# Attention of two batches ahead of a SwiGLU FFN: a new load order, and down projections held back, in a fused one-core kernel

## Chip, cores, metric

One core of one Trainium2 chip. The metric is the device time of one execution in microseconds (us). Medians are quoted with their range; every comparison is made by ratio to runs of the kernel before.

## The reference

Block-causal attention over 8 batches, 8 heads, 576 tokens and head size 64, then a root-mean-square norm and a SwiGLU FFN on 4608 tokens of width 512 with an inner width of 1536. Everything comes and goes in float32.

```python
scores = (q @ k^T) / sqrt(64)             # token i sees token j if i//64 >= j//64
x      = softmax(scores) @ v              # (8, 8, 576, 64) -> (4608, 512)
xn     = x / sqrt(mean(x*x) + 1e-6) * rms_g
g      = xn @ w_gate
out    = (g * sigmoid(g) * (xn @ w_val)) @ w_out
```

## The kernel before

The kernel emits its own schedule: the order of the Python calls is the order of the instructions on each engine. Tiles carry the waits. The parts that matter:

```python
NST = 6                                         # staging tiles for loads (fp32)
nat    = pool(bufs=10)                          # bf16 tiles after the cast on GpSimd
ps_s   = pool(bufs=2)   # PSUM: scores, values    ps_f = pool(bufs=4)   # PSUM: FFN, norm, transposes

def issue(): ...        # next load of the list `todo`, on Sync's queue
def cast(eng, n=1):     # oldest staged tile to bf16, then issue() into the freed staging tile
    ...
def transpose_pair(b, t): ...  # TensorE transposes, VectorE copies to QT/KT     (batches 0 and 1)
def transpose_dma(b, c):  ...  # DMA transposes on Sync's queue                  (other batches)
def scores(b, t, step):   ...  # 3 steps a head pair; exp on ScalarE; corner memsets on VectorE

def values(b, t, early=False):
    ...                                         # 10 matmuls into ov[:, 0, :]
    out(OT[b][:, t, 0:512], SQ[b][:, t, 0:512], ov[:, 0, :])    # two ScalarE passes
    if t == HP - 1:
        for u in range(HP):                     # end blocks, into ov[:, 1, :] of the same tile
            for a in range(2):
                nc.tensor.matmul(ov[a*D:(a+1)*D, 1, u*BLK:(u+1)*BLK], ...)
        out(OT[b][:, :, 512:S], SQ[b][:, :, 512:S], ov[:, 1, 0:HP*BLK]...)

def ffn_up(n, m):   ...  # 8 matmuls, tanh on ScalarE, two multiplies on VectorE
def ffn_down(n, i): ...  # 12 matmuls, ScalarE copy to osb, then
    nc.sync.dma_start(out=out[rows[0]:rows[0] + P, :], in_=osb)

def group():             # one FFN step: a down if due, else an up if its tokens are normed, else a down
    ready = di < len(downs) and (ui == len(ups) or downs[di][0]*NMC + NMC + 2 <= ui)
    if ready and (ui == len(ups) or 3*di <= ui - NMC - 3): ffn_down(*downs[di]); di += 1
    elif ui < len(ups) and <last batch of the chunk> < scaled: ffn_up(*ups[ui]); ui += 1
    elif di < len(downs) and downs[di][0]*NMC + NMC <= ui: ffn_down(*downs[di]); di += 1
    gone += 1; <run what `later` has set for this count>

def tail(b):             # norm of a batch, spread over the next five groups
    norm_sums(b, 0); norm_sums(b, 1); later(1, norm_root, b)
    for u in range(HP + 1): later(3 + u//2, norm_scale, b, u)
    later(3 + HP//2, mark, b)                   # only now may up steps use batch b
```

The order before: attention of batch 0 (up weights issued beside its V), norm of batch 0 with nothing beside it, then FFN groups between the attention steps of batches 1 to 7. A group without a step that may run is empty.

The softmax here doesn't subtract the row's maximum and nothing guards it: scores larger than these inputs give would overflow.

## Time and profile before

| | before |
|---|---|
| time, 2 runs | 441.5 us (441.24 to 441.77) |
| profiled span | 441.4 us, mean granted clock 0.974 |
| TensorE busy | 388.4 us (88%) |
| loads, transposes and stores on Sync's queue | 45.9 MB |

The prediction below quotes the page, the table of stretches and TensorE's timeline, and says how to read them. In a timeline line the numbers are the start, the length, then what ran, and in brackets how long the engine had been idle and who ended it.

### The profile page before, as it was taken

The page shows a single profiled execution, that of the slowest core. Times are in us where ns is not written, and L with a number is a line of the kernel's source. Part 1 is how long each engine was busy: PE and PEld are TensorE (multiplying, and loading weights), DVE is VectorE, ACT ScalarE, POOL GpSimd, SP SyncE. Part 2 cuts the span into 40 slices and gives each one's busy share as a digit, 9 for nine tenths or more (in the row PEclk, how much of TensorE's full clock was granted, in tenths as well). Part 3 has the DMA queues.
Part 4 walks back from the last instruction along what each step waited for, and adds up shares of the span by engine and source line. Part 5 has one row for each costly group of instructions (what it writes and reads, how often), then busy time and mean ns, then how long its engine had stood idle before and what let it go on. Part 6 is the DMA issues. An engine that isn't in the chain of part 4 may idle for free.

```text
span 441.4 us, 7178 instructions
## 1 busy us (share of the span) xinstructions
PE 388.4 (88%) x2661; PEld 172.7 (39%) x2704; DVE 249.0 (56%) x593; ACT 216.3 (49%) x322; POOL 86.1 (20%) x138
## 2 busy tenths in 40 slices
PE   3535679985998999899989998999899989999995
PEld 1213343332344434443444444444444444444442
DVE  4615875506665466546654665566546665776430
ACT  3503147643765466546754675467546732333221
POOL 2547243332241023201320232011000000000000
PEclk9999589997999999999999999999999999999998
DMA  8999999987990499349936982492011002000012
GB/s 207 166 233 228 209 194 147 188 206 150 169 185 0 108 202 173 57 107 192 182 57 105 197 184 55 107 185 43 1 61 37 1 0 73 24 1 24 24 50 95
DMA packets 142708, 51.08 MB, mean 116 GB/s; under 512 B 129360, under 2 KB 138064, under 8 KB 142672
## 3 DMA queue, kind: packets, MB, share of 16 engines
q1 hardware_dynamic: 136320, 45.89, 51.4%
q0 software_dynamic: 5824, 4.72, 6.8%
q8 instruction: 21, 0.34, 0.3%
q14 instruction: 15, 0.12, 0.1%
q10 hardware_dynamic: 528, 0.00, 0.1%
HBM read 38.80 MB, written 9.44 MB: 109 GB/s over the span
## 4 chain that ended last, share of the span: by engine, by line
PE 81%; DMA 7%; ACT 4%; DVE 4%; POOL 1%; issue 1%; SPq 0%; DVEq 0%; POOLq 0%; ACTq 0%
PE fps L415 22%; PE fps L431 21%; PE fps L419 21%; PE sps L248 6%; PE sps L288 4%; DMA st<-in_k_dram 3%; DMA st<-in_v_dram 2%; PE fps L324 2%; ACT PT L254 2%; DMA WO<-in_moe_w_out_dram 2%; PE fps L396 2%; ACT SQ L299 1%; DVE QT L222 1%; ACT OT L298 1%; DVE KT L222 1%
## 5 line engine op out<-in xcount | busy, mean ns | idle before, releaser
L254 ACT ACTIVATE PT<-sps 128x1024 bf16<-128x1024 f32 (+1 forms) x96 | 93.9, 988 | 66.7 <-PE sps L248 65.7
L424 DVE SCALAR_TENSOR_TENSOR gs<-th,fps 128x512 bf16<-128x512 f32 x108 | 74.3, 688 | 75.4 <-ACT th L422 74.7
L415 PE MATMUL fps<-XT,WG 128*128 128x512 bf16 x408 | 111.0, 385 | 1.5 <-issue 0.5
L419 PE MATMUL fps<-XT,WV 128*128 128x512 bf16 x430 | 112.1, 383 | 0.2
L431 PE MATMUL fps<-WO,HT 128*128 128x512 bf16 x417 | 96.9, 379 | 0.8
L422 ACT ACTIVATE th<-fps 128x512 f32<-128x512 f32 x108 | 64.9, 601 | 64.9 <-PE fps L415 62.8
L426 DVE TENSOR_TENSOR HT<-gs,fps 128x512 bf16<-128x512 bf16 x108 | 74.2, 687 | 11.5 <-PE fps L419 0.4
L419 PEld LDWEIGHTS <-WV 128*128 128x128 bf16 x432 | 42.7, 99 | 52.3 <-issue 2.3
L431 PEld LDWEIGHTS <-HT 128*128 128x128 bf16 x432 | 40.7, 98 | 49.8 <-issue 3.5
L145 POOL CAST nt<-st 128x512 bf16<-128x512 f32 (+1 forms) x60 | 36.8, 615 | 111.9 <-DMA st<-in_k_dram 88.7
L434 ACT ACTIVATE osb<-fps 128x512 f32<-128x512 f32 x36 | 21.5, 597 | 71.7 <-PE fps L431 58.7
L415 PEld LDWEIGHTS <-WG 128*128 128x128 bf16 x432 | 37.2, 98 | 47.1 <-issue 11.7
L389 DVE SCALAR_TENSOR_TENSOR XT<-OT,gscale,fps 128x64 bf16<-128x64 bf16 (+3 forms) x72 | 30.2, 476 | 30.8 <-PE fps L396 27.7
L248 PE MATMUL sps<-QT,KT 64*128 64x512 bf16 (+3 forms) x256 | 38.4, 341 | 3.3 <-DVE KT L222 1.6
L288 PE MATMUL sps<-PT,VB 128*64 128x512 bf16 (+3 forms) x256 | 27.3, 338 | 0.0
L138 POOL CAST VB<-st 128x512 bf16<-128x512 f32 x24 | 14.8, 615 | 53.3 <-DMA st<-in_v_dram 50.6
L248 PEld LDWEIGHTS <-KT 64*128 64x128 bf16 x256 | 9.9, 94 | 35.2 <-issue 31.0
L288 PEld LDWEIGHTS <-VB 128*64 128x64 bf16 x320 | 13.8, 114 | 22.9 <-POOL VB L140 8.7
L299 ACT ACTIVATE SQ<-sps 128x512 bf16<-128x512 f32 (+1 forms) x37 | 20.9, 565 | 2.9 <-DVE OT L293 2.9
L298 ACT CAST OT<-sps 128x512 bf16<-128x512 f32 (+1 forms) x35 | 18.8, 538 | 4.3 <-PE sps L306 2.8
L396 PE MATMUL fps<-st,SELB 128*128 128x512 bf16 x30 | 10.2, 426 | 7.9 <-DVE st L378 7.6
L215 PE MATMUL fps<-ident,nt 96*128 96x96 bf16 x96 | 7.7, 246 | 8.4 <-DVE nt L128 7.9
(69 smaller groups left out, 184.9 us busy)
## 6 DMA issues: line engine op xcount, KB each, us to landing
out_dram<-osb SPq DMA_DIRECT2D x28, 256.0 KB, 2.3
st<-in_q_dram SPq DMA_DIRECT2D x24, 256.0 KB, 4.5
st<-in_k_dram SPq DMA_DIRECT2D x24, 256.0 KB, 4.9
st<-in_v_dram SPq DMA_DIRECT2D x24, 256.0 KB, 4.0
st<-in_v_dram SPq DMA_DIRECT2D x32, 128.0 KB, 5.3
st<-in_q_dram SPq DMA_DIRECT2D x8, 288.0 KB, 6.6
st<-in_k_dram SPq DMA_DIRECT2D x8, 288.0 KB, 7.0
out_dram<-osb SPq DMA_DIRECT2D x16, 128.0 KB, 2.4
```

Of the source, the lines that this page charges most:

```text
L145: eng.tensor_copy(out=nt[0:r, 0:512], in_=st[0:r, 0:512])
L248: nc.tensor.matmul(sp[:, a, o:o + CH_W[c]], KT[b][r, t, c * P:(c + 1) * P], QT[b][r, t, CH_Q[c]:S], start=True, stop=True, skip_group_chec ...
L254: nc.scalar.activation(out=pt[:, :, lo:lo + width], in_=sp[:, :, 0:width], func=AF.Exp, scale=SCALE)
L288: nc.tensor.matmul(ov[a * D:(a + 1) * D, 0, 512 - w:512], vb[:, c, h * D:(h + 1) * D], rhs, start=(c == 4), stop=(c == 3), skip_group_chec ...
L299: nc.scalar.activation(out=sq, in_=i, func=AF.Square)
L389: nc.vector.scalar_tensor_tensor(out=XT[:, u, y0:y0 + hi - lo], in0=OT[b][:, u, j0 + lo:j0 + hi], scalar=gscale[:, u:u + 1], in1=src[:, lo ...
L415: nc.tensor.matmul(g, WG[m // 3][:, p, (m % 3) * P:(m % 3 + 1) * P], XT[:, p, x0:x0 + TOKC], start=(p == 0), stop=(p == HP - 1))
L419: nc.tensor.matmul(u, WV[m // 3][:, p, (m % 3) * P:(m % 3 + 1) * P], XT[:, p, x0:x0 + TOKC], start=(p == 0), stop=(p == HP - 1))
L422: nc.scalar.activation(out=th, in_=g, func=AF.Tanh, scale=0.5)
L424: nc.vector.scalar_tensor_tensor(out=gs, in0=th, scalar=1.0, in1=g, op0=ALU.add, op1=ALU.mult)
L426: nc.vector.tensor_mul(out=HT[n][:, m, :], in0=gs, in1=u)
L431: nc.tensor.matmul(po, HT[n][:, m, i * P:(i + 1) * P], WO[:, m, :], start=(m == 0), stop=(m == NMC - 1))
```

## The change

Its intent: fill the thin first 112 us. Batch 0's V no longer shares the DMA engines with weights; the attention of batches 0 and 1 fills TensorE while the weights arrive; batch 2 is loaded and transposed as batches 0 and 1 are; the down projections wait for weights that come last.

```diff
-    def issue():
+    def issue(behind=None):            # optionally waits for a weight tile before the load
-            todo += [("vp", b, t) for t in range(HP)] + [("v", b, 4)]
+            todo += [("v", b, 4)] + [("vp", b, t) for t in range(HP)]    # and for 3 batches, not 2
@@ scores: corner memsets are gathered and issued a group later
-            nc.vector.memset(pt[BLK:P, :, 512:512 + BLK], 0.0)
+            corners.append((gone, pt[BLK:P, :, o:o + BLK]))
@@ values: end-block matmuls come before the copies; batch 0 uses ps_f instead of ps_s
-        out(OT[b][:, t, 0:512], SQ[b][:, t, 0:512], ov[:, 0, :])
+        outs = [(OT[b][:, t, 0:512], SQ[b][:, t, 0:512], ov)]
         if t == HP - 1:
             ... end-block matmuls ...
-            out(...)
+            outs.append(...)
+        for o, sq, i in outs: <copy and square>
@@ norm_root
-        for i in range(3):
+        for i in range(2):
@@ group
-        ready = di < len(downs) and downs[di][0]*NMC + NMC + 2 <= ui       # (cut)
+        ready = di < len(downs) and downs[di][0]*NMC + NMC + 2 <= ui and ui >= DOWN0    # DOWN0 = 20
@@ order (cut)
+    <attention of batch 0, batch 1's transposes and scores between its pieces, norm of batch 0>
+    cast(nc.gpsimd, 2, refill=False); load_up(0); load_up(1)
+    cast(nc.gpsimd, 3, refill=False); load_up(2); load_up(3)
+    <rest of batch 1's scores, values(1, 0..2)>; group(); values(1, 3); later(1, tail, 1)
+    while len(flying) < NST: issue(behind=WV[3][0:1, 0, 0:1])     # batch 2 behind the up weights
+    group(6)
+    for t in range(HP):                 # batch 2: transposes, scores, values; 16 groups between
+        if t < 3: transpose_pair(2, t)
+        if t == 2: transpose_pair(2, 3); scores_ends(2)
+        ...                             # load_out (down weights) at t == 2, step 1
+    values(2, 3); later(1, tail, 2)
+    later(1, transpose_dma, 3, 0)       # batch 3's DMA transposes start here
+    for _ in range(6):
+        group(); fetch(3); fetch(3)     # fetch: cast on GpSimd; every second one a DMA transpose
     <batches 3 to 7 as before>
```

More of the change, by code (lines that the diff above doesn't have):

```diff
@@ L54 @@
     NST = 6
+    NPE = 3
     const = ctx.enter_context(tc.tile_pool(name="const", bufs=1))
@@ L98, in issue @@
         st = stage.tile([P, 6 * P], FP32, name="st")
+        if behind is not None:
+            nc.gpsimd.tensor_copy(out=st[0:1, 0:1], in_=behind)
         src = {"q": q, "k": k, "v": v}[kind[0]]
@@ L119, in issue, with cast @@
         flying.append(((kind, b, i), st))
-    def cast(eng, n=1):
+    def cast(eng, n=1, refill=True):
         for _ in range(n):
@@ L145, in cast @@
                 eng.tensor_copy(out=nt[0:r, 0:512], in_=st[0:r, 0:512])
-            issue()
+            if refill:
+                issue()
     for b in range(B):
-        if b < 2:
+        if b < NPE:
             for t in range(HP):
                 todo += [("qp", b, t), ("kp", b, t)]
-            todo += [("vp", b, t) for t in range(HP)] + [("v", b, 4)]
+            todo += [("v", b, 4)] + [("vp", b, t) for t in range(HP)]
         else:
@@ L233, with clear @@
     PT, P4, OT, SQ = {}, {}, {}, {}
+    corners = []
+    gone = 0
+    def clear(age=0):
+        while corners and corners[0][0] <= gone - age:
+            nc.vector.memset(corners.pop(0)[1], 0.0)
     def scores(b, t, step):
@@ L255, in scores @@
                              func=AF.Exp, scale=SCALE)
-        if step == 1:
-            nc.vector.memset(pt[BLK:P, :, 512:512 + BLK], 0.0)
-        if step == 2:
-            for o in (960, 1280):
-                nc.vector.memset(pt[BLK:P, :, o:o + BLK], 0.0)
+        for o in ((), (512,), (960, 1280))[step]:
+            corners.append((gone, pt[BLK:P, :, o:o + BLK]))
     def scores_ends(b):
@@ L281, in values @@
         vb = VB[b % NV]
-        ov = ps_s.tile([P, 2, 512], FP32, name="sps")
+        if early:
+            ov = ps_f.tile([P, 512], FP32, name="fps")
+            oh = ps_f.tile([P, 512], FP32, name="fps") if t == HP - 1 else None
+        else:
+            ob = ps_s.tile([P, 2, 512], FP32, name="sps")
+            ov, oh = ob[:, 0, :], ob[:, 1, :]
         for c in (4, 0, 1, 2, 3):
@@ L287, in values @@
                 w = CH_W[c] if c < 4 else BLK
-                nc.tensor.matmul(ov[a * D:(a + 1) * D, 0, 512 - w:512],
+                nc.tensor.matmul(ov[a * D:(a + 1) * D, 512 - w:512],
                                  vb[:, c, h * D:(h + 1) * D], rhs,
                                  start=(c == 4), stop=(c == 3), skip_group_check=True)
-        def out(o, sq, i):
-            if early:
-                nc.vector.tensor_copy(out=o, in_=i)
-                if t < HP - 1:
-                    nc.vector.tensor_mul(out=sq, in0=o, in1=o)
-                    return
-            else:
-                nc.scalar.copy(out=o, in_=i)
-            nc.scalar.activation(out=sq, in_=i, func=AF.Square)
-        out(OT[b][:, t, 0:512], SQ[b][:, t, 0:512], ov[:, 0, :])
+        outs = [(OT[b][:, t, 0:512], SQ[b][:, t, 0:512], ov)]
         if t == HP - 1:
@@ L305, in values @@
                     h = 2 * u + a
-                    nc.tensor.matmul(ov[a * D:(a + 1) * D, 1, u * BLK:(u + 1) * BLK],
+                    nc.tensor.matmul(oh[a * D:(a + 1) * D, u * BLK:(u + 1) * BLK],
                                      vb[:, 5, h * D:(h + 1) * D], P4[b][:, a, u, :],
                                      start=True, stop=True, skip_group_check=True)
-            out(OT[b][:, :, 512:S], SQ[b][:, :, 512:S],
-                ov[:, 1, 0:HP * BLK].rearrange("p (t d) -> p t d", t=HP))
+            outs.append((OT[b][:, :, 512:S], SQ[b][:, :, 512:S],
+                         oh[:, 0:HP * BLK].rearrange("p (t d) -> p t d", t=HP)))
+        for o, sq, i in outs:
+            if early:
+                nc.vector.tensor_copy(out=o, in_=i)
+                nc.vector.tensor_mul(out=sq, in0=o, in1=o)
+            else:
+                nc.scalar.copy(out=o, in_=i)
+                nc.scalar.activation(out=sq, in_=i, func=AF.Square)
     nrm = {}
@@ L446, in ffn_down @@
                                   in_=osb[j * BLK:(j + 1) * BLK, :])
-    late_constants()
-    def casts_early(t):
-        cast(nc.vector)
-        cast(nc.gpsimd)
-    casts_early(0)
-    transpose_pair(0, 0, k_on_act=True)
-    scores(0, 0, 0)
-    casts_early(1)
-    scores(0, 0, 1)
-    transpose_pair(0, 1)
-    scores(0, 0, 2)
-    casts_early(2)
-    scores(0, 1, 0)
-    scores(0, 1, 1)
-    transpose_pair(0, 2)
-    casts_early(3)
-    scores(0, 1, 2)
-    load_up(0)
-    transpose_pair(0, 3)
-    scores(0, 2, 0)
-    cast(nc.gpsimd, 1)
-    load_up(1)
-    scores_ends(0)
-    cast(nc.gpsimd, 4)
-    scores(0, 2, 1)
-    values(0, 0, early=True)
-    scores(0, 2, 2)
-    values(0, 1, early=True)
-    scores(0, 3, 0)
-    scores(0, 3, 1)
-    values(0, 2, early=True)
-    scores(0, 3, 2)
-    norm_sums(0, 0)
-    values(0, 3, early=True)
-    norm_sums(0, 1)
-    load_up(2)
-    load_up(3)
-    norm_root(0)
-    for t in range(HP + 1):
-        norm_scale(0, t)
-    pairs = [(b, t) for b in range(1, B) for t in range(HP)]
     ups = [(n, m) for n in range(NTC) for m in range(NMC)]
     downs = [(n, i) for n in range(NTC) for i in range(4)]
-    ui = di = gone = 0
-    scaled = 1
+    ui = di = 0
+    scaled = 0
     due = []
+    DOWN0 = 20
     def later(after, fn, *args):
@@ L504, in mark, with group @@
         scaled = b + 1
-    def group():
+    def group(n=1):
         nonlocal ui, di, gone
-        ready = di < len(downs) and (ui == len(ups) or downs[di][0] * NMC + NMC + 2 <= ui)
-        if ready and (ui == len(ups) or 3 * di <= ui - NMC - 3):
-            ffn_down(*downs[di])
-            di += 1
-        elif ui < len(ups) and min(B - 1, ((ups[ui][0] + 1) * TOKC - 1) // S) < scaled:
-            ffn_up(*ups[ui])
-            ui += 1
-        elif di < len(downs) and downs[di][0] * NMC + NMC <= ui:
-            ffn_down(*downs[di])
-            di += 1
-        gone += 1
-        now = [d for d in due if d[0] <= gone]
-        due[:] = [d for d in due if d[0] > gone]
-        for _, fn, args in now:
-            fn(*args)
+        for _ in range(n):
+            ready = di < len(downs) and downs[di][0] * NMC + NMC + 2 <= ui and ui >= DOWN0
+            if ready and (ui == len(ups) or 3 * di <= ui - NMC - 3):
+                ffn_down(*downs[di])
+                di += 1
+            elif ui < len(ups) and min(B - 1, ((ups[ui][0] + 1) * TOKC - 1) // S) < scaled:
+                ffn_up(*ups[ui])
+                ui += 1
+            elif di < len(downs) and downs[di][0] * NMC + NMC <= ui:
+                ffn_down(*downs[di])
+                di += 1
+            gone += 1
+            clear(1)
+            now = [d for d in due if d[0] <= gone]
+            due[:] = [d for d in due if d[0] > gone]
+            for _, fn, args in now:
+                fn(*args)
     def tail(b):
@@ L531, in tail, with pair_in @@
         later(3 + HP // 2, mark, b)
-    cast(nc.gpsimd, 2)
-    group()
-    cast(nc.gpsimd, 2)
-    transpose_pair(1, 0)
-    cast(nc.gpsimd, 2)
-    group()
-    transpose_pair(1, 1)
-    cast(nc.gpsimd, 2)
-    for m in range(0, NMC, 3):
-        load_out(m, 3)
-    cast(nc.gpsimd, 5)
-    fetched = []
+    late_constants()
+    def pair_in(b, t):
+        cast(nc.vector if b == 0 else nc.gpsimd)
+        cast(nc.gpsimd)
+        transpose_pair(b, t, k_on_act=(b == 0 and t == 0))
+    pair_in(0, 0)
@@ new lines @@
+    scores(0, 0, 0)
+    scores(0, 0, 1)
+    pair_in(0, 1)
+    scores(0, 0, 2)
+    scores(0, 1, 0)
+    pair_in(0, 2)
+    scores(0, 1, 1)
+    scores(0, 1, 2)
+    pair_in(0, 3)
+    clear()
+    scores(0, 2, 0)
+    cast(nc.gpsimd, 5)
+    scores(0, 2, 1)
+    scores_ends(0)
+    scores(0, 2, 2)
+    clear()
+    values(0, 0, early=True)
+    scores(0, 3, 0)
+    values(0, 1, early=True)
+    scores(0, 3, 1)
+    pair_in(1, 0)
+    values(0, 2, early=True)
+    scores(0, 3, 2)
+    scores(1, 0, 0)
@@ new lines @@
+    clear()
+    norm_sums(0, 0)
+    values(0, 3, early=True)
+    norm_sums(0, 1)
+    scores(1, 0, 1)
+    pair_in(1, 1)
+    scores(1, 0, 2)
+    norm_root(0)
+    scores(1, 1, 0)
+    pair_in(1, 2)
+    scores(1, 1, 1)
+    for u in range(HP + 1):
+        norm_scale(0, u)
+    mark(0)
+    scores(1, 1, 2)
+    pair_in(1, 3)
+    clear()
+    scores(1, 2, 0)
+    cast(nc.gpsimd, 2, refill=False)
+    for j in range(2):
+        load_up(j)
+    cast(nc.gpsimd, 3, refill=False)
+    for j in range(2, 4):
+        load_up(j)
@@ new lines @@
+    scores_ends(1)
+    scores(1, 2, 1)
+    scores(1, 2, 2)
+    scores(1, 3, 0)
+    scores(1, 3, 1)
+    clear()
+    scores(1, 3, 2)
+    values(1, 0)
+    values(1, 1)
+    values(1, 2)
+    group()
+    clear()
+    values(1, 3)
+    later(1, tail, 1)
+    while len(flying) < NST:
+        issue(behind=WV[3][0:1, 0, 0:1])
+    cast(nc.gpsimd, 2)
+    group(6)
+    for t in range(HP):
+        if t < 3:
+            transpose_pair(2, t)
+        if t == 2:
+            transpose_pair(2, 3)
+            scores_ends(2)
+        for step in range(3):
+            scores(2, t, step)
+            if t == 2 and step > 0:
+                values(2, step - 1)
+            if t == 3 and step == 1:
+                values(2, 2)
+            if step == 0:
+                cast(nc.gpsimd, (2, 4, 3, 2)[t])
+            if t == 2 and step == 1:
+                cast(nc.gpsimd, 2)
+                for m in range(0, NMC, 3):
+                    load_out(m, 3)
+            group()
+        group()
@@ L548, in fetch @@
+    values(2, 3)
+    later(1, tail, 2)
+    fetched = 2
     def fetch(b):
-        n = len(fetched)
-        if n < 15 and b < B:
+        nonlocal fetched
+        if fetched < 15 and b < B:
             cast(nc.gpsimd)
-            fetched.append(n)
-            if n % 2 == 1 and n < 10:
-                later(1, transpose_dma, b, n // 2)
-    for idx, (b, t) in enumerate(pairs):
-        prev = pairs[idx - 1] if idx else None
-        if t == 0:
-            del fetched[:]
-            if b == 1:
-                scores(b, 0, 0)
-                group()
-                transpose_pair(1, 2)
-                scores(b, 0, 1)
-                group()
-                transpose_pair(1, 3)
-                scores(b, 0, 2)
-                scores_ends(1)
-                group()
-                continue
+            fetched += 1
+            if fetched % 2 == 0 and fetched <= 10:
+                later(1, transpose_dma, b, fetched // 2 - 1)
@@ L572 @@
+    later(1, transpose_dma, 3, 0)
+    for _ in range(6):
+        group()
+        fetch(3)
+        fetch(3)
+    pairs = [(b, t) for b in range(3, B) for t in range(HP)]
+    for b, t in pairs:
+        if t == 0:
+            while fetched < 15:
+                fetch(b)
+            fetched = 0
             scores_ends(b)
@@ L574 @@
         scores(b, t, 0)
-        if prev:
-            values(*prev)
-            if prev[1] == HP - 1:
-                later(1, tail, prev[0])
+        if (b, t) != pairs[0]:
+            values(*((b, t - 1) if t else (b - 1, HP - 1)))
+            if t == 0:
+                later(1, tail, b - 1)
         fetch(b + 1)
@@ L586 @@
         scores(b, t, 2)
-        group()
-        if b > 1:
-            group()
+        group(2)
         fetch(b + 1)
```

## The prediction

> **What bounds the kernel now.** I began with the page: TensorE's share of the span, then the row of forty slices, to see whether that share is even.
>
> ```profile
> PE 388.4 (88%) x2661; PEld 172.7 (39%) x2704; DVE 249.0 (56%) x593; ACT 216.3 (49%) x322; POOL 86.1 (20%) x138
> PE   3535679985998999899989998999899989999995
> GB/s 207 166 233 228 209 194 147 188 206 150 169 185 0 108 202 173 57 107 192 182 57 105 197 184 55 107 185 43 1 61 37 1 0 73 24 1 24 24 50 95
> ```
>
> TensorE is the bound, but not evenly. A slice is 11.04 us; slices 1 to 6 and the tenth (99 to 110 us) are thin, everything later is full. The table by stretches says how much:
>
> ```profile
> 0.00:20.00 20.00, 8.84 (x82) 4.80 (x83) 12.05 (x47) 8.59 (x10) 8.56 (x17) 1.00 0.92 186
> 20.00:50.00 30.00, 12.47 (x131) 6.38 (x132) 12.86 (x37) 6.34 (x9) 15.63 (x21) 0.88 1.23 225
> 50.00:112.00 62.00, 52.16 (x391) 22.70 (x395) 32.38 (x75) 31.70 (x47) 19.11 (x31) 0.89 0.95 179
> 112.00:441.40 329.40, 314.97 (x2062) 138.86 (x2094) 191.76 (x436) 169.64 (x259) 42.81 (x70) 1.00 0.44 89
> ```
>
> The first number after the length is TensorE's busy time. It does 21.3 us of work in the first 50 us, loses 9.8 us from 50 to 112 at a granted clock of 0.89, and from 112 us on is 96% busy at full clock. Only the first 112 us have anything to give. TensorE's timeline there names the holes (start, length, what, and in brackets the idle time before and who ended it):
>
> ```profile
> 28.95 0.27 PE L288 MATMUL sps<-P,VB 128*64 128x64 bf16 x2 [8.27 <-POOL VB L140]
> 47.28 1.44 PE L396 MATMUL fps<-st,SELB 128*128 128x512 bf16 x3 [3.65 <-DVE st L378]
> 49.37 1.90 PE L415 MATMUL fps<-XT,WG 128*128 128x512 bf16 x4
> 107.47 1.04 PE L396 MATMUL fps<-st,SELB 128*128 128x512 bf16 x2 [3.92 <-DVE st L378]
> ```
>
> First, batch 0's values wait for V until 28.95 us, because the up weights were fetched beside V. Second, the norm of batch 0 (a chain of small VectorE instructions) stands bare until 47.28, and the first up projection starts at 49.37. Third, batch 1's norm stands bare again at 100 to 112 us: the twelve up steps of the first 512 tokens were used up by 84.6 us and the next chunk needs batch 1.
>
> **What the Trainium skill says.** "DMA: Bandwidth & Descriptors", section "Issuing engines are not separate DMA queues", says transfers issued from Sync and GpSimd interleave on the same 16 engines. The trace agrees: with weights in flight, the cast of V's last tile waits until 28.29 us, although V was issued from 7.9 us. "TensorE: Matmul & The Clock Gate", Part 1, says TensorE runs at half clock after an idle window of about 3.4 us. The trace agrees in kind: the four matmuls at 49.37 took 1.90 us, those at 53.49 1.03. The same page ("Architectural detail") calls VectorE's queue strict FIFO; for a delayed copy this is what makes everything behind it late, and I build my start time on it. "SBUF — State Buffer", section "SBUF: two separate sides", describes a port pair that VectorE and GpSimd lock against each other: VectorE's cast of 96x768 took 1.22 us beside a GpSimd cast at 12.92, and 0.55 alone.
>
> **The change, part by part.**
>
> *Load order.* A batch is 8 loads of 288 KB for q and k and 10 of 128 KB for V, 3.67 MB (decimal) in all; the up weights are 8 x 384 KB = 3.15 MB. Summing the GB/s row (each x 11.04 us): 2.3, 4.1, 6.7, 9.2, 11.5, 13.6, 15.2, 17.3, 19.6 MB by the ends of slices 1 to 9. Now batch 0 is whole at about 18 us (V was 29), batch 1 at about 35, the first up weights at 39 and the last (10.5 MB) at 50. Down weights come behind batch 2 and six tiles of batch 3 (18.9 MB): about 96 us.
>
> *When the first up step starts.* It now stands behind all of batch 1's scores and three of its values, so the queue of VectorE and then ScalarE decides, not the weights. Values of batch 0 can start at about 20 us (scores of three pairs are ahead of them, ScalarE-paced, 1.02 and 0.92 us each from 9.2 us). From values to the transposes of the norm sums took 28.95 to 40.60 = 11.7 us; the same again gives 32, as what is interleaved fills holes. Then VectorE has, in its strict order: norm sums 2.1 (40.60 to 42.70), copies of pair 1 of batch 1 1.5 (two of 0.75), root 2.9 (43.67 to 47.23, less one iteration of 3 x 0.21), copies of pair 2 1.5, scaling 3.5 (47.91 to 51.40), copies of pair 3 1.5. Sum 13.0: 45 us. The end scores need that last copy, and in ScalarE's order the end exponentials (0.6) and five wide ones (3 x 1.02 + 2 x 0.92) follow: 50.5. Values that wait for two score buffers add 2.5. **First up step at about 53 us**, against 49.4 before, but with batch 1's attention done.
>
> *What is left from there.* TensorE at full clock, from durations of before: an up step is 8 x 0.216 = 1.73 us, a down step 12 x 0.216 = 2.59. The steady period of one batch is 44.27 us (sums at 140.33, 184.60, 228.86) and holds 12 ups and 4 downs, so attention with its norm costs 44.27 - 20.7 - 10.4 = 13.1. After 436.8 us (last matmul) come 4.7 us of copy and store. Check on before from 112.17 us, with 96 ups, 32 downs and 5.6 batches left: 165.9 + 82.9 + 73.4 + 4.7 = 326.9, real 329.2; I carry the 2.3. From 49.4 us the same sum says 49.4 + 279.9 + 7 x 13.1 + 2.6 (transposes) + 4.7 + 2.3 = 430.6, real 441.4. So **10.8 us** are holes and cold clock between 49 and 112 us.
>
> After: 53 + 186.6 (108 ups) + 93.3 (36 downs) + 4.8 (rest of batch 1: last values 1.25, norm 3.5) + 6 x 13.1 + 2.6 (batch 2's transposes, now on TensorE) + 4.7 + 2.3 = **425.9**.
>
> *New cost.* In the first seven up steps VectorE has 7 x 1.48 (two of 0.69 with gaps), batch 1's norm 8.5 and copies 1.5 = 20.4 us, TensorE 12.1 + 4.8 = 16.9: about 3 us of waiting, in which a cold start at half clock hides. Sum **429 us**.
>
> *Small parts.* One Newton iteration less is 0.6 us a batch, and beyond batch 0 it lies beside matmuls. Corner memsets (96 x 0.11) only move. Holding the downs to up step 20 costs no work: eight ups of chunk 1 fill the gap, as batch 1's norm is ready after seven groups. The first down comes at about 53 + 34.6 + 4.8 + 2.6 + 8 + 3 = 106 us, ten after its weights. So the hole at 100 to 112 should go: batch 2's norm has four downs of chunk 0, three ups and some downs of chunk 1 beside it.
>
> **The rivals.** *Start chain shorter*: if VectorE's copies and the norm of batch 0 overlap better, TensorE starts at 47 us and the result is 423. For it: VectorE is busy only 12.86 of 30 us now, and ScalarE has 20 us of slack. Against: one queue in order, and I have already counted it without holes from 32 to 45. *Loads bind*: the up weights land at 50 on my sum; at the 166 GB/s of slice 2 they would land near 60, the down weights past 106, and the time would be 434 to 438. For it: DMA is busy 0.9 and more to 112 us. Against: q and k rows in the order of batches 0 and 1 are longer, and slices with them moved 228 GB/s. *The moved attention is paid back*: VectorE and the four FFN accumulators hold TensorE through the first twenty steps, and the clock falls to half; 6 to 10 us, so 432 to 436. For it: before, between 61.8 and 66 us, just such copies caused a 2 us hole and half clock after it. Against: the copies of batch 2 now come one pair at a time with up steps between.
>
> **Range and chances.** The largest error is the start (plus or minus 5), then the VectorE waits (minus 3 to plus 6). I predict 429 us, 420 to 437 in eight of ten. Faster by over 2% means below about 432.8: 0.72. Within 2%: 0.27. Slower: 0.01, since the work is conserved and only a late load could stretch it by 9 us.
>
> **What would show it.** Values of batch 0 at about 20 us instead of 28.95; first up step between 48 and 57 us with batch 1's values before it; no idle piece over 2 us on TensorE after it, the norm of batch 1 and 2 hidden; the first down at about 106 us not released by a load; steady period 44.3 us and an end of 4.7 us unchanged. It would be wrong if the first up waits for a weight, if TensorE runs at half clock for longer than 4 us after the start, or if the down projections wait for their weights.

## The result, and the profile after

The changed kernel is correct and **slower**: 453.72 us (453.49 to 453.95), against 441.5. The ratio is 1.0277 (95% interval 1.0232 to 1.0321).

Two rows of the page of the kernel after (40 slices of 11.3 us, busy tenths):

```profile
PE   3776886988997399996999999999999999999995
DMA  8999999900028899837990699187002001100012
```

The first slices of TensorE are fuller than before, as intended. But there is a thin place in the thirteenth and fourteenth slices and another in the nineteenth, and the DMA engines stand nearly still in slices 9 to 11, in a kernel that is still loading. TensorE's timeline of the kernel after, at the places that the prediction named and at its largest waits:

```profile
19.45 0.27 PE L301 MATMUL fps<-P,VB 128*64 128x64 bf16 x2
52.65 1.21 PE L425 MATMUL fps<-XT,WG 128*128 128x512 bf16 x4
69.33 0.38 PE L406 MATMUL fps<-st,SELB 128*128 128x512 bf16 x1 [2.55 <-DVE gs L434]
79.59 0.39 PE L259 MATMUL sps<-QT,KT 64*128 64x512 bf16 x2 [2.48 <-DVE KT L227]
92.13 0.39 PE L259 MATMUL sps<-QT,KT 64*128 64x512 bf16 x2 [2.20 <-DVE KT L227]
118.98 2.76 PE L441 MATMUL fps<-WO,HT 128*128 128x512 bf16 x12
154.29 0.43 PE L278 MATMUL sps<-QT,KT 64*64 64x64 bf16 x16 [8.63 <-DMA KT<-nt]
212.14 1.03 PE L406 MATMUL fps<-st,SELB 128*128 128x512 bf16 x2 [3.08 <-DVE st L388]
```

Batch 0's values start at 19.45 us (predicted 20) and the first up step at 52.65 (predicted 53). All of the miss lies behind that point: 376 us were forecast from there to the end, 399.4 were needed. The waits fall into three kinds: 1.1 to 2.6 us on VectorE between 66 and 105 us (four pieces), 8.63 us on batch 3's K, and a bare norm of batch 3 at 206 to 217 us.

The largest one has its cause some 60 us earlier, and TensorE's own timeline cannot show it. This is Sync's queue (the second number runs from the start of an issue to its end, and over the gaps where a line holds several):

```profile
80.54 4.22 SPq L115 DMA_DIRECT2D st<-in_k_dram  x1
122.41 8.68 SPq L452 DMA_DIRECT2D out_dram<-osb  x3
131.19 1.32 SPq L234 DMA_TRANSPOSE QT<-nt  x1
```

and GpSimd, whose casts feed the transposes and set the next loads free:

```profile
100.69 1.17 POOL L149 CAST nt<-st 128x512 bf16<-128x512 f32 x2 [9.78 <-PE fps L220]
137.02 0.61 POOL L149 CAST nt<-st 64x512 bf16<-64x512 f32 x1 [35.16 <-DMA st<-in_q_dram]
```

Sync issues nothing from 84.8 to 122.4 us. Its next instruction in program order is the store of the first down projection, which waits for it; the three stores go at 122 to 131 us, and only then come batch 3's transposes and the rest of its loads, although eight of its loads had been issued by 84.8 us. GpSimd waits 35.16 us for a tile whose load stands behind those stores.

In the kernel before the order was the other way round. There the last of batch 2's ten transposes is issued ahead of the first store:

```profile
87.79 1.23 SPq L229 DMA_TRANSPOSE KT<-nt  x1
90.36 0.87 SPq L442 DMA_DIRECT2D out_dram<-osb  x1
```

### The profile page after: what moved, and what is told of

Same layout as the page of the kernel before. It is cut to its first block, busy times and chain, and to the rows that moved or that the text cites. A ratio compares the mean times of both kernels' runs of the same rounds, so it can differ in the third digit from the quotient of the medians.

```text
span 452.1 us, 7299 instructions
## 1 busy us (share of the span) xinstructions
PE 403.6 (89%) x2752; PEld 177.8 (39%) x2752; DVE 252.2 (56%) x579; ACT 213.9 (47%) x320; POOL 86.4 (19%) x141
## 4 chain that ended last, share of the span: by engine, by line
PE 77%; DVE 13%; DMA 3%; ACT 3%; SPq 2%; issue 1%; POOL 0%; DVEq 0%; ACTq 0%; POOLq 0%
PE fps L425 21%; PE fps L441 20%; PE fps L429 18%; PE sps L259 6%; PE sps L301 5%; DMA st<-in_k_dram 2%; PE fps L334 2%; DVE QT L227 2%; DVE HT L436 2%; DVE gs L434 1%; DVE KT L227 1%; PE fps L406 1%; DVE XT L399 1%; ACT PT L265 1%; SPq L234 1%
## 5 line engine op out<-in xcount | busy, mean ns | idle before, releaser
L425 PE MATMUL fps<-XT,WG 128*128 128x512 bf16 x432 | 114.8, 389 | 0.0
L429 PE MATMUL fps<-XT,WV 128*128 128x512 bf16 x432 | 113.6, 386 | 0.0
L149 POOL CAST nt<-st 128x512 bf16<-128x512 f32 (+1 forms) x50 | 30.2, 612 | 136.0 <-DMA st<-in_q_dram 63.7
L259 PE MATMUL sps<-QT,KT 64*128 64x512 bf16 (+3 forms) x256 | 41.1, 365 | 7.9 <-DVE KT L227 5.7
L301 PE MATMUL sps<-PT,VB 128*64 128x512 bf16 (+1 forms) x224 | 24.8, 347 | 0.9 <-DVE PT L244 0.9
L301 PEld LDWEIGHTS <-VB 128*64 128x64 bf16 x320 | 14.8, 119 | 16.2 <-issue 10.1
L142 POOL CAST VB<-st 128x512 bf16<-128x512 f32 x20 | 12.2, 612 | 41.6 <-DMA st<-in_v_dram 30.3
L132 POOL CAST nt<-st 96x768 bf16<-96x768 f32 x20 | 16.5, 824 | 19.1 <-DMA st<-in_k_dram 15.3
L406 PE MATMUL fps<-st,SELB 128*128 128x512 bf16 x32 | 11.6, 444 | 9.0 <-DVE st L388 4.9
```

What stands on the lines that cost most here:

```text
L149: eng.tensor_copy(out=nt[0:r, 0:512], in_=st[0:r, 0:512])
L259: nc.tensor.matmul(sp[:, a, o:o + CH_W[c]], KT[b][r, t, c * P:(c + 1) * P], QT[b][r, t, CH_Q[c]:S], start=True, stop=True, skip_group_chec ...
L301: nc.tensor.matmul(ov[a * D:(a + 1) * D, 512 - w:512], vb[:, c, h * D:(h + 1) * D], rhs, start=(c == 4), stop=(c == 3), skip_group_check=True)
L425: nc.tensor.matmul(g, WG[m // 3][:, p, (m % 3) * P:(m % 3 + 1) * P], XT[:, p, x0:x0 + TOKC], start=(p == 0), stop=(p == HP - 1))
L429: nc.tensor.matmul(u, WV[m // 3][:, p, (m % 3) * P:(m % 3 + 1) * P], XT[:, p, x0:x0 + TOKC], start=(p == 0), stop=(p == HP - 1))
```

## The experiments

Two of the rivals to this reading are tested below: GpSimd's ten bf16 tiles (the line with 9.78 us is a wait for one of those), and loads that are simply too many.

**Summary** (ratio to the kernel before; the columns of three stretches, in us of the span, are TensorE's busy time in the profile, left empty where not asked):

| run | us (median, range) | ratio (95%) | 52:106 | 106:160 | 160:220 |
|---|---|---|---|---|---|
| before, with the result | 441.50 (441.24-441.77) | 1 | 46.0 | 50.5 | 58.3 |
| after | 453.72 (453.49-453.95) | 1.0277 (1.0232-1.0321) | 42.3 | 44.0 | 55.5 |
| e1: stores on ScalarE | 445.27 (444.01-446.58) | 1.0015 (0.9967-1.0064) | 41.5 | 51.9 | 54.3 |
| e3: hold to step 16 | 453.94 (451.65-455.36) | 1.0205 (1.0151-1.0259) | 42.0 | 44.0 | 55.1 |
| e9: transposes ahead | 443.61 (443.48-445.3) | 0.9983 (0.9900-1.0066) | 42.6 | 51.9 | 54.7 |
| e6: e1, two groups | 439.18 (438.29-440.1) | 0.9878 (0.9801-0.9955) | 42.4 | 52.5 | 59.0 |
| e7: e1, K copies on ScalarE | 440.10 (437.77-442.15) | 0.9890 (0.9804-0.9977) | 45.0 | 51.7 | 53.7 |
| e8: e1, transposes hoisted | 437.08 (435.3-438.72) | 0.9823 (0.9747-0.9900) | 48.1 | 51.9 | 54.2 |
| c1: all three mended | 425.88 (423.79-427.29) | 0.9587 (0.9538-0.9636) | 49.3 | 52.0 | 59.4 |
| c2: c1, norm spread | 424.91 (423.54-427.91) | 0.9564 (0.9514-0.9614) | 49.2 | 51.9 | 59.4 |
| e2: before, stores on ScalarE | 453.66 (452.75-456.27) | 1.0214 (1.0149-1.0279) | | | |
| e5: before, end blocks first | 434.04 (432.14-435.25) | 0.9759 (0.9709-0.9808) | | | |
| e10: before, load order | 447.64 (445.73-449.18) | 1.0064 (1.0016-1.0112) | | | |
| c3: before, order and end blocks | 435.82 (435.11-437.81) | 0.9815 (0.9763-0.9867) | | | |

The kernel before ran at medians of 445.08 us beside e1, e2, e3 and e5, and of 444.15 beside e6 to e9. For c1 to c3 and e10 the record lists twelve runs of it, median 444.57, of which eleven are those of the other two sessions. The changed kernel itself was timed only with the result. So differences between kernels of different sessions are taken between ratios.

A verdict asks whether a kernel is clear of 2%: after is slower, c1 and c2 are faster, e1, e6, e7, e9 and e10 are within 2% of before. The intervals of e2, e3, e5, e8 and c3 lie off 1 but reach across 2%, and their verdict is unclear.

### e1: the stores leave Sync's queue

```diff
-            nc.sync.dma_start(out=out[rows[0]:rows[0] + P, :], in_=osb)
+            nc.scalar.dma_start(out=out[rows[0]:rows[0] + P, :], in_=osb)     # both stores of ffn_down
```

> The changed kernel with the output stores issued from ScalarE's queue instead of Sync's. Theory A: Sync's queue takes its instructions in order, and the first three output stores (which wait for the first down projections at 122 us) stand ahead of batch 3's transposes and of its remaining loads, so the DMA engines idle from 85 to 122 us and TensorE waits 8.63 us at 145.7, then runs at half clock for about 2 us more. It expects DMA traffic without that hole, no wait for KT at about 145 us, and 442 to 445 us (453.7 less 9 to 11). Rival B (the ten nat buffers hold GpSimd back, whatever Sync does): the wait stays, 452 to 455. Rival C (the bytes of batch 3 simply come too late): the wait shrinks to some us, 447 to 451. All expect the bare norm of batch 3 (about 5 us at 206 to 217 us) to stay, since the order of the instructions on TensorE is the same.

Measured: 445.27 us; the ratio falls from 1.0277 to 1.0015, some 11 us. (e3, which keeps the stores on Sync, took 453.94 us in the same session.) Sync's queue in this run:

```profile
81.65 4.21 SPq L115 DMA_DIRECT2D st<-in_k_dram  x1
85.96 2.86 SPq L234 DMA_TRANSPOSE QT<-nt  x1
```

The transpose follows the load at once, 45 us earlier than in the kernel after. No wait for batch 3's K is left in TensorE's timeline, and its busy time in the stretch 106:160 rises from 44.0 to 51.9 us. Nothing about the ten bf16 tiles or the bytes was changed, so rivals B and C fall. The bare norm of batch 3 stays (2.69 us idle ahead of its scaling), as expected.

### e2: the control

The same edit in the kernel before.

> Control: the kernel before with the output stores on ScalarE's queue. Theory A: no store stands ahead of a load that matters there, so 440 to 443 us, the same as before. If it is clearly faster, the queue also cost the kernel before something, and the gain of the previous run is not the change's debt alone.

Measured: 453.66 us, 2.1% slower (1.5 to 2.8%). The expectation missed, and it taught something. ScalarE in this run:

```profile
90.82 0.36 ACTq L442 DMA_DIRECT2D out_dram<-osb  x1
91.23 1.02 ACT L254 ACTIVATE PT<-sps 128x1024 bf16<-128x1024 f32 x1 [5.64 <-DMA st<-in_k_dram]
```

The copy that the store writes out was done at 85.59 us, but the store goes only at 90.82. The trace puts the wait down to a load of K, which the store does not need by its data; why it waits for one is not shown. The exponential behind the store on ScalarE waits too: 5.64 us here and 4.31 at 100.7. So a store can block whichever of the two engines issues it. Moving it to ScalarE was no mend in itself; in e1 the first three stores happened to go within 0.1 us of their copies (at 122.30, 125.32 and 130.64).

### e3: a shorter hold

```diff
-    DOWN0 = 20
+    DOWN0 = 16
```

> The changed kernel with the down projections held to up step 16 instead of 20 (the earliest place behind the issue of the down weights). Theory A: the first store leaves about 10 us earlier (near 110 instead of 122 us), so Sync is free earlier, the 8.63 us wait for batch 3 falls to nothing or 1 us, and the time is 443 to 446 us. Rival D (the hold is harmless, the loads are late for another reason): 452 to 455. If the down weights were late, the first down would show a wait for a load.

Measured: 453.94 us, against e1's 445.27 in the same session; its interval overlaps that of the kernel after. Sync's queue, then TensorE's third down projection and its wait:

```profile
112.42 0.37 SPq L452 DMA_DIRECT2D out_dram<-osb  x1
...
120.10 10.74 SPq L452 DMA_DIRECT2D out_dram<-osb  x2
130.94 1.33 SPq L234 DMA_TRANSPOSE QT<-nt  x1
```

```profile
127.06 2.76 PE L441 MATMUL fps<-WO,HT 128*128 128x512 bf16 x12
153.78 0.43 PE L278 MATMUL sps<-QT,KT 64*64 64x64 bf16 x16 [8.38 <-DMA KT<-nt]
```

The first store went 10 us earlier, as expected, and let two loads through. But three stores stand ahead of the transposes, and the third waits for a down projection that still ends at 130 us. The expectation was wrong about which store counts: the last one ahead of the transposes. The hold does not move that one. The other rule in `group()`, `3*di <= ui - NMC - 3`, which the kernel before has too, lets the third down (di = 2) go only at up step 21. By that rule it is the 24th group with a hold of 20, of 16, or with none, and the first transposes are written behind that group. The trace agrees: the third down starts at 127.06 us here and at 127.33 in the kernel after. So it is not the hold that put stores ahead of the transposes, but where the change wrote the transposes. A run without any hold was not made, since the down weights are issued only behind group 16.

### e9: the transposes go ahead of the stores

The stores stay on Sync. Only the place in the program of batch 3's casts (each of which also issues a load) and transposes changes.

```diff
             group()
         group()
+        if t == 2:
+            for c in range(5):
+                cast(nc.gpsimd, 2)
+                transpose_dma(3, c)
     values(2, 3)
-    fetched = 2
+    fetched = 10
-    later(1, transpose_dma, 3, 0)
```

> The changed kernel with its stores left on Sync's queue, but batch 3's ten casts and its DMA transposes written in the program behind step 2 of batch 2's pairs, so that they stand ahead of the first three output stores in Sync's queue. Theory A (Sync's order): as with the stores moved away, no wait for KT near 145 us, DMA traffic from 85 to 122 us, 444 to 446 us against 453.7. If the stores mattered in another way than by their place in the queue, the wait stays and it is 450 or more.

Measured: 443.61 us, ratio 0.9983, no wait for K, 51.9 us busy in 106:160. Sync's queue now has the last transpose ahead of the three stores, which go no earlier than in the kernel after:

```profile
104.47 1.24 SPq L234 DMA_TRANSPOSE KT<-nt  x1
121.88 8.68 SPq L452 DMA_DIRECT2D out_dram<-osb  x3
```

With the same stores on the same queue, order alone removed the loss. Together with e1 this settles the largest term.

### e6: two groups instead of six ahead of batch 3 (on top of e1)

```diff
-    for _ in range(6):
-        group(); fetch(3); fetch(3)
+    for _ in range(2):
+        fetch(3); fetch(3); fetch(3); fetch(3); group()
```

> e1_after_store_act with two FFN groups instead of six ahead of batch 3's scores. Theory F: in the changed kernel five of the groups beside batch 3's norm are empty, because the FFN steps that batch 2 allows have been spent, so the norm stands bare (5 us of idle and slow clock near 200 us). Counting groups, with two ahead only one of the five is empty. It expects no idle over 1 us near that norm, and 4 to 5 us less than e1: 440 to 441 where e1 has 445.3. Rival: batch 3 then is not loaded in time and waits for KT; no gain or a loss.

Measured: 439.18 us, ratio 0.9878 against e1's 1.0015: 1.4%, 6 us. The stretch 160:220 goes from 54.3 to 59.0 us busy, the others barely move, and no idle piece over 0.5 us is left at that norm. Its first scaling now has no wait ahead of it, where e1 had 2.69 us:

```profile
194.75 0.59 PE L406 MATMUL fps<-st,SELB 128*128 128x512 bf16 x2
```

The up steps of the next chunk need batch 3 whole; the four extra groups had spent the steps that could have lain beside its norm. Nobody waits for an instruction there: the instruction is missing from the program, which is why the wait is put down to the norm itself.

### e7 and e8: VectorE in the first twenty up steps (on top of e1)

```diff
-            transpose_pair(2, t)
+            transpose_pair(2, t, k_on_act=True)          # e7: K copies on ScalarE
```

```diff
-    group(6)
+    group(5); transpose_pair(2, 0); group()              # e8: pair 0; pairs 1 to 3 likewise, one or two groups earlier (cut)
```

> e1_after_store_act with the K copies of batch 2's four transposed pairs on ScalarE instead of VectorE. Theory G: VectorE's queue (norm of batch 1, two multiplies per up step, copies) holds TensorE in the first twenty up steps: idle of 2.19, 2.48, 2.20 and 1.11 us between 68 and 104 us in e1, each followed by some us at half clock. It expects the three waits for KT to fall to about 0.8 to 1.5 us and 3 to 5 us less than e1: 440 to 442. Rival: TensorE then waits for ScalarE instead; same as e1.

> e1_after_store_act with batch 2's four transposed pairs each written one FFN group earlier, so that a group of TensorE work lies between a transpose and the scores that need its copies. Theory G says the waits for KT (2.48, 2.20, 1.11 us) go, with the half clock behind them: 5 to 7 us less than e1, 438 to 440. Rival: VectorE is full there whatever the order, so the wait moves to the accumulators and the gain is under 2 us.

Measured: e7 440.10 us (ratio 0.9890, 1.2% less than e1), e8 437.08 (0.9823, 1.9% less). The interval of e7 touches that of e1, so its gain in time alone is not clear of noise. In e7 the two long waits shrank to 1.81 and 1.53 us and moved to the Q copy; in e8 two short ones are left of the three, of 0.62 and 0.40 us:

```profile
86.77 0.39 PE L259 MATMUL sps<-QT,KT 64*128 64x512 bf16 x2 [0.62 <-DVE KT L227]
```

The stretch 52:106 rises from 41.5 us busy to 45.0 and 48.1. So it was less VectorE's sum than its place: scores stood directly behind the transposes whose copies VectorE had yet to reach in its queue. Rival "VectorE is full whatever the order" falls for these waits.

### e5: the end blocks first, in the kernel before

```diff
-        out(OT[b][:, t, 0:512], SQ[b][:, t, 0:512], ov[:, 0, :])
         if t == HP - 1:
             ... end-block matmuls ...
+        out(OT[b][:, t, 0:512], SQ[b][:, t, 0:512], ov[:, 0, :])
+        if t == HP - 1:
             out(OT[b][:, :, 512:S], SQ[b][:, :, 512:S], ...)
```

> The kernel before with one part of the change alone: the end-block values are multiplied before the copies of the main block are issued, so they no longer wait for the copies that read the same tile. The profile of before shows 8 waits of 1.2 to 1.5 us there (10.7 us together), and the steady period of a batch is 44.27 us before and 42.76 after. Theory E: the period becomes 42.8 to 42.9, and the time 430 to 433 us. Rival: the wait is filled by another one and the time stays at 440 to 442.

Measured: 434.04 us, ratio 0.9759, 2.4% faster than before (1.9 to 2.9%); 1 us above the top of what was expected, on a chip on which before itself ran 3.6 us slower. The end blocks of two batches in the kernel before, and its table of waits (us in total, times, longest):

```profile
182.45 0.32 PE L306 MATMUL sps<-P,VB 128*64 128x64 bf16 x8 [1.32 <-ACT SQ L299]
226.72 0.32 PE L306 MATMUL sps<-P,VB 128*64 128x64 bf16 x8 [1.32 <-ACT SQ L299]
```

```profile
PE sps L306 <- ACT SQ L299: 10.7, 8, 1.5
```

and with the edit, from TensorE's timeline:

```profile
223.08 0.29 PE L305 MATMUL sps<-P,VB 128*64 128x64 bf16 x8
265.84 0.29 PE L305 MATMUL sps<-P,VB 128*64 128x64 bf16 x8
```

The wait is gone and the period of a batch is 42.76 us instead of 44.27. The matmuls wrote a half of the tile that nobody read, but they waited for the readers of the other half. This part of the change is a clear gain, and the changed kernel has it too; the rest of the change lost all of it and more.

### e10 and c3: the load order, in the kernel before

```diff
-    load_up(0)
     transpose_pair(0, 3)
     scores(0, 2, 0)
     cast(nc.gpsimd, 1)
-    load_up(1)
     scores_ends(0)
     cast(nc.gpsimd, 4)
+    load_up(0)
+    load_up(1)
```

> The kernel before with the load order alone: the first two up weight blocks are issued behind batch 0's V instead of beside it. The hole of 8.27 us ahead of batch 0's values goes (values at about 20 instead of 29 us), the norm of batch 0 follows 8 us earlier, and the first up step starts at 41 to 44 us instead of 49.4. Theory (what follows is TensorE-bound, so an earlier start is an earlier end): 437 to 440. Rival (batch 1's loads come later and its norm stays bare, so the gain is lost by 112 us): 442 to 445, no change.

> The kernel before with two parts of the change alone: the load order of the previous run and the end blocks first (434.0 alone). If both gains are real and separate, 427 to 431; if the load order gives nothing, 434.

Measured: e10 447.64 us (1.0064), c3 435.82 (0.9815 against e5's 0.9759). TensorE in e10:

```profile
42.10 1.90 PE L415 MATMUL fps<-XT,WG 128*128 128x512 bf16 x4
...
61.99 0.22 PE L288 MATMUL sps<-P,VB 128*64 128x64 bf16 x2 [3.32 <-POOL VB L140]
...
91.55 0.43 PE L270 MATMUL sps<-QT,KT 64*64 64x64 bf16 x16 [4.81 <-DMA KT<-nt]
...
111.08 1.03 PE L396 MATMUL fps<-st,SELB 128*128 128x512 bf16 x2 [4.14 <-DVE st L378]
```

The first up step starts 7 us earlier, and by 112 us all of it is given back: TensorE waits for batch 1's V and batch 2's K, and batch 1's norm is as bare as before. In this stretch a load brought forward puts another one back. The order of loads by itself is worth nothing; it needs work to put in the freed place.

### c1 and c2: the three mends together

c1 is the changed kernel with e9's order, two groups ahead of batch 3, batch 2's transposes hoisted and their K copies on ScalarE. c2 spreads batch 1's norm scaling over five groups as well.

```diff
-            later(3 + u // 2, norm_scale, b, u)
+            later(3 + (u if b == 1 else u // 2), norm_scale, b, u)      # c2 only
```

> The changed kernel with three mends together: batch 3's casts and transposes ahead of the first stores (stores left on Sync), two groups instead of six ahead of batch 3's scores, and batch 2's transposes a group earlier with their K copies on ScalarE. If the three costs are separate, the gains seen one by one add: 443.6 (transposes ahead) less 6 (two groups, 445.3 to 439.2) less 8 (hoisted, 445.3 to 437.1) less 1 = 428 to 431, against 444 to 445 for before and 434 for before with the end blocks first. If they share one wait, it stops at 435 to 437.

> The same with batch 1's norm scaling spread over five groups instead of two and a half. Theory G (VectorE is full in the first seven up steps): the last hole of 2.2 us near 68 us goes, 1 to 3 us less than c1. Rival: VectorE's sum is the same and only moves the wait, within 1 us of c1.

Measured: c1 425.88 us, ratio 0.9587; c2 424.91, 0.9564, not apart from c1 (the rival's case: the hole near 68 us is still 2.11 us). The page of c1:

```profile
PE   3776786999999999999999999999999999999995
```

The thin places behind the start are gone but for the one near 68 us, and the gains added, a little better than expected. c1 and c2 are the fastest kernels, 4% under before and 1.7 to 2% under e5.

## Why the prediction was wrong

Forecast 429 us and faster, measured 453.7 and slower. Point by point:

- **What bounds the kernel, and the start**: right. The holes were where the prediction read them, values came at 19.45 us (20 forecast) and the first up step at 52.65 us (53), by the VectorE and ScalarE queues as worked out. (Batch 0 "whole at about 18 us" is 19.4 by the prediction's own bytes.) A weight was never waited for, and the clock in the first 13 us behind the start was full (0.99).
- **"The hole at 100 to 112 should go"**: right for the norm of batch 2 (no idle piece over 0.75 us), nearly so for that of batch 1 (2.55 us), wrong as a general statement. Groups were counted for those two batches and not for batch 3, whose norm stood bare instead: about 6 us by e6.
- **The failed step: the load order, and with it "only a late load could stretch it", at a chance of 0.01.** The prediction added bytes, and asked of each load only when the DMA engines could carry it. It never asked when Sync, which takes its list in order, could issue it. So the sum from the first up step on has 6 x 13.1 for the later batches and no wait for batch 3's K. The program of the changed kernel, which was there before the prediction, has three stores ahead of batch 3's transposes and the rest of its loads; the kernel before has the transposes of batch 2 ahead of its first store. The third store waits for a down projection that ends at 130 us, and TensorE then stood 8.63 us for K. It cost about 11 us (e1, e9). The rival "loads bind" named the loads for the wrong reason: the DMA engines were idle, the issue was blocked.
- **"Holding the downs to up step 20 costs no work"**: not refuted. A hold of 16 gave no clear gain (e3), and the store that counts does not move with the hold. The first down came at 118.98 us and not at 106, behind the waits of the next point, and it waited for no load.
- **"New cost: about 3 us of waiting"** in the first seven steps: the mechanism was right, the size too small. It is the prediction's rival "the moved attention is paid back", and larger than the 6 to 10 us put down there (15.8 by the ledger below). The trace has 11.6 us of idle between 52.65 and 112 us (pieces of 2.55, 2.48, 2.20, 1.11 and smaller), and three up steps at half clock, some 4 us more. Two terms were missed: the scores that stand directly behind batch 2's transposes (e8: 8 us), and VectorE's root of batch 1's norm, which took 4.8 us instead of the 2.9 forecast (63.89 to 68.71).
- **"Steady period 44.3 us unchanged"**: wrong, to the good. The diff moves the end-block matmuls ahead of the copies, and the prediction passed over it. The profile of before listed the wait (10.7 us over 8 batches); e5 shows it worth some 11 us over the whole kernel.
- **The ledger** behind the first up step, from the trace: 15.8 us of idle and half clock up to 112 us, about 12 at batch 3's K (8.63 idle, 1.4 just before, some 2 at half clock), about 6 at batch 3's norm, less 9 for six periods of 1.5 us. That is 25 us, of which the prediction had 5.3 (3 and the carried 2.3), so 19.5 are new; the miss was 23.4. It closes to within 4 us; the half-clock parts are estimated from matmul lengths in this trace (1.86 and 1.59 us where 1.03 is full speed).

What stays open: why a store on ScalarE waited for a load (e2), and the last wait of 2.1 us near 68 us in c1 and c2.

## What to carry to other kernels

When a change writes loads, transposes or stores in a new order, read the list of the queue that carries them: a store that waits for a compute step blocks every later load and transpose on that queue, and the bill comes tens of microseconds later on another engine. A schedule that runs work ahead must also count what is left to lie beside each later serial chain. And a table of waits is worth reading for small regular entries: here a reordering of four lines (e5) was worth some 11 us, nearly the 12.5 that the prediction expected of the whole change.

## What the Trainium skill lacked or had wrong

- "DMA: Bandwidth & Descriptors", section "Issuing engines are not separate DMA queues", says that initiating DMAs on several engines saves only the sequencer's issue time. That section does not say that a DMA that waits holds back all that stand behind it on the engine that issues it, and here this decided far more: with stores and loads on Sync, Sync issued nothing for 37.6 us (84.8 to 122.4), and moving the stores took the ratio from 1.0277 to 1.0015; in the kernel before the same move cost 2.1%.
- No page that was looked up says that a store can wait for a load whose data it does not need. In e2 ScalarE stood 5.64 and 4.31 us at a store, released, by the trace, by loads of k and q; the reason is not shown.
- "TensorE: Matmul & The Clock Gate", Part 1, gives an idle window of about 3.4 us for the fall to half clock. In the kernel after, up steps ran at half clock behind idle pieces of 2.55 and 2.48 us (1.86 us for four matmuls instead of 1.03). Single gaps shorter than the stated window, in a stretch that is thin anyway, were enough. No length of one gap decides it: behind 2.20 us the clock stayed full in this kernel (1.04 us for four at 92.45) and fell in e1 (1.77 at 91.52).
- "SBUF — State Buffer", section "SBUF: two separate sides", says that the one of VectorE and GpSimd that comes second to their shared ports fully blocks. The runs agree, and the section could stress small instructions: one step of the norm's root on 18 columns took 0.80 us at 64.10 us in the kernel after, to 0.04 us behind the end of a GpSimd cast, and 0.18 at 34.21. The first was part of a root of 4.8 us.
